# Natural head order, loads on two queues by time of use, unchained list scatters, a GpSimd mask and ranks by matmul in a DeltaNet block with routed experts

## The chip, the core and the metric

The kernel runs on one core of one Trainium2 chip. The metric is the device time of one execution in microseconds (us), as the median of several runs. A core has five engines with an instruction queue each: TensorE (PE in the profile; its weight loads are PEld), VectorE (DVE), ScalarE (ACT), GpSimd (POOL) and SyncE (SP), which here only issues DMAs. Each queue runs in order: an instruction that waits holds up all behind it, DMA issues included. DMAs move data between HBM and the on-chip SBUF; matmul results land in PSUM, from which VectorE and ScalarE copy them.

## The reference, cut to what matters

```python
def _attn_ref(q, k, v, beta):                     # B, H, S, D = 4, 8, 768, 48
    k_n = k / (np.linalg.norm(k, axis=-1, keepdims=True) + 1e-06)
    state = np.zeros((B, H, D, D))
    for t in range(S):
        y[:, :, t] = einsum('bhd,bhde->bhe', q[:, :, t], state)
        v_old = einsum('bhde,bhd->bhe', state, kt)
        state = state + bt * einsum('bhd,bhe->bhde', kt, vt - v_old)

# x = y in the order (B*S, H*D): 3072 tokens of 384
def _moe_ref(x, expert_emb, tau, w1, w2):         # E = 8 experts, F = 1024
    logits = xn @ en.T / tau                      # xn, en: rows over their norms
    expert_idx = np.argmax(logits, axis=1)
    gate_w = softmax(logits)[np.arange(N), expert_idx]
    for e in range(E):
        mask = expert_idx == e
        h = np.maximum(x[mask] @ w1[e], 0.0)
        out[mask] = gate_w[mask, None] * (h @ w2[e])
```

A delta-rule recurrence over 768 time steps gives 3072 tokens; each goes to the one expert whose embedding it is nearest to in angle.

## The kernel before, in words

Time is cut into 12 chunks of C = 64 steps. The four sequences are two pairs (`p`); a tile holds the two sequences of a pair in the two halves of its 128 partitions (`g`), 64 steps each, and the eight heads side by side.

For each chunk: `load` and `load_q` fetch keys (twice: `K` for the norms and products, `Kl` for the state update), values and queries; `squares`, `root`, `inverse_norms` and `unit_keys` scale the keys (GpSimd and VectorE); `transposes` puts keys and queries head by head on the partitions (TensorE, ScalarE); `products` multiplies the keys with keys and queries of the chunk (TensorE), and VectorE masks both to earlier steps into the tile `AP` (L263). The key products' 32-step diagonal blocks go through HBM (`blocks_out` L271, `blocks_in` L276) into `Bk`, one matrix per partition, for two chunks at once; `weigh` scales them by beta on GpSimd (L282); `eliminate` inverts the triangular matrices in 31 pairs of VectorE instructions (L290, L292), handed out a few at a time by `steps(n)`; `inverses_back` brings the inverses `Tk` back through HBM, `turn` transposes them, and `lower1` and `lower2` finish the 64-step inverse `W`. Then the recurrence itself: `residual` (values less what the state gives for the keys, L337 and L348), `solve` (with `W`, L357), `update` and `keep` (the state), `outputs`, `store`, and the router's `logits`.

The main loop runs c from -6 to 11 and is a hand-made pipeline under a manual schedule: in one iteration it works on norms of chunk c+6, products of chunk c+5, `lower1` and `lower2` of chunk c+1 and the recurrence of chunk c. Every two chunks share one reload and one elimination: the reload stands at the end of an even iteration, the elimination starts in the odd iteration behind it. What the source says first, each engine runs first. All loads and stores of this stage are issued by SP, in source order; ScalarE issues 16 small loads of beta at the start (L152).

After every fourth chunk `route` picks the experts of 1024 tokens in eight columns (`J`), as a generator of small steps that `fill(n)` advances: softmax, first maximum, then the place of each token in its expert's list: two matmuls give the ranks within a column (`mask_su`) and the counts of a column (`ones`), and eight pairs of VectorE additions carry the running count from column to column (L470, L471). Eight indirect DMAs from GpSimd (L482) scatter the token numbers into the list `idmap`; each is taken as depending on the one before it, since all write the same tensor.

Then the expert stage: 19 tiles of 256 list places. `fetch` reads a piece of `idmap` (L638), the expert's weights, and gathers the tokens (L646); `experts` multiplies (L657 to L670) and scatters the rows of the result. The first list read waits for all scatters.

Of the kernel before, what the change touches and what calls it, by code (L numbers as in the profile page):

```python
# [21 lines left out]
def kernel(  # L22
# [75 lines left out]
    run = cpool.tile([128, E], F32, name="run")  # L98
# [12 lines left out]
    for i in range(P2):  # L111
        Qs.append(ac.tile([128, NP, 2, 64], F32, name=f"Qp{i}"))
        nc.gpsimd.memset(Qs[i], 0.0)
        KNs.append(ac.tile([128, NP, 2, 64], F32, name=f"KN{i}"))
        nc.gpsimd.memset(KNs[i], 0.0)

    def heads(t):

        return t.rearrange("p (a b) d -> p b a d", a=2)

    def load(src, c, name, bufs):
        ts = []
        for p in range(P2):
            t = wk.tile([128, H, D], F32, name=name, tag=name, bufs=bufs)
            for g in range(2):
                nc.sync.dma_start(out=t[64 * g:64 * g + 64],
                                  in_=src[2 * p + g, :, c * C:(c + 1) * C, :].rearrange("h t d -> t h d"))
            ts.append(t)
        return ts

    def load_q(c):
        for p in range(P2):
            for g in range(2):
                for hh in range(2):
                    nc.sync.dma_start(out=Qs[p][64 * g:64 * g + 64, :, hh, 0:D],
                                      in_=q[2 * p + g, hh * NP:(hh + 1) * NP, c * C:(c + 1) * C, :]
                                      .rearrange("h t d -> t h d"))
# [5 lines left out]
    Kf[1] = load(k, 1, "K", 4)  # L143
# [83 lines left out]
    def unit_keys(c):  # L227
        for p in range(P2):
            nc.gpsimd.tensor_tensor(KNs[p][:, :, :, 0:D], heads(Kf[c][p]),
                                    rns[c][:, p].rearrange("p (a b) -> p b a", a=2).unsqueeze(3)  # L230
                                    .broadcast_to([128, NP, 2, D]), op=ALU.mult)
        del Kf[c]
# [7 lines left out]
    def transposes(c, p, i):  # L240
        if i == 0:
            KQs[c, p] = wk.tile([128, NP, 2, 2, C], F32, name="KQ", tag="KQ", bufs=12)
        src = (KNs, Qs)[i][p]
        psT = bank("f", 3).rearrange("p (a n) -> p a n", a=NP)
        for hp in range(NP):
            nc.tensor.transpose(psT[:, hp], src[:, hp].rearrange("p a d -> p (a d)"), ident)  # L246
        nc.scalar.activation(KQs[c, p][:, :, :, i, :], psT.rearrange("p a (g t) -> p a g t", g=2), ACT.Copy)  # L247

    def products(c, p):

        if p == 0:
            APs[c] = wk.tile([128, P2, 2, NP, 2, C], F32, name="AP", tag="AP", bufs=6)
# [9 lines left out]
        for hh in range(2):  # L262
            nc.vector.tensor_tensor(APs[c][:, p, hh].rearrange("p a i t -> p (a i) t"),  # L263
                                    psG[hh].rearrange("p (a t) -> p a t", t=C),
                                    later.broadcast_to([128, 2 * NP, C]), op=ALU.mult)

    def blocks_out(c):
        s, i = c // 2, c % 2
        A = APs[c].rearrange("p a b c i t -> p (a b c) i t")
# [8 lines left out]
    def weigh(s):  # L278
        Tks[s] = wk.tile([128, Q, Q], F32, name="Tk", tag="Tk")
        nc.gpsimd.memset(Tks[s], 0.0)  # L280
        nc.gpsimd.tensor_copy(Tks[s].rearrange("p a b -> p (a b)")[:, 0:Q * Q:Q + 1], bb[:, s])
        nc.gpsimd.tensor_tensor(Bks[s], Bks[s], bb[:, s].unsqueeze(1).broadcast_to([128, Q, Q]), op=ALU.mult)  # L282
# [23 lines left out]
    def lower1(c):  # L306
# [4 lines left out]
        A = APs[c].rearrange("p a b c i t -> p (a b c) i t")  # L311
# [29 lines left out]
    def residual(c, p):  # L341
        V = Vl[c][p]
        if c == 0:
# [4 lines left out]
        nc.vector.tensor_tensor(heads(R), heads(V),  # L348
                                psK[:, 0:Dm].rearrange("p (b a d) -> p b a d", a=2, d=D), op=ALU.subtract)
# [12 lines left out]
    def update(c, p):  # L362
        for hp in range(NP):
            for g in range(2):
                for hh in range(2):
                    h = hh * NP + hp
# [9 lines left out]
    def outputs(c, p):  # L376
# [4 lines left out]
        for hp in range(NP):  # L381
            for hh in range(2):
                for g in range(2):
                    r = slice(64 * g, 64 * g + 64)
                    o = 2 * D * hp + D * hh
                    nc.tensor.matmul(psY[r, o:o + D], lhsT=A[r, p, hh, hp, 1, :], rhs=Zs[p][r, hh * NP + hp, :],
                                     start=(c == 0 and hp == 0 and hh == 0), stop=True, skip_group_check=True)
        if p == 0:
            xcs[c] = wk.tile([128, P2, Dm], F32, name="xc", tag="xc", bufs=3)
        nc.scalar.activation(xcs[c][:, p].rearrange("p (a b d) -> p b a d", a=2, d=D),  # L390
                             psY[:, 0:Dm].rearrange("p (b a d) -> p b a d", a=2, d=D), ACT.Copy)
# [30 lines left out]
    def route(b):  # L422
# [29 lines left out]
        psR = bank("f", 3)[:, 0:2 * J * E].rearrange("p (i a e) -> p i a e", i=2, e=E)  # L452
# [13 lines left out]
        rk = t("rk", [128, 2, J, E])  # L466
        nc.vector.tensor_copy(rk, psR)
# [5 lines left out]
        nc.vector.tensor_tensor(rk[:, 0], rk[:, 0], base_e.broadcast_to(be), op=ALU.add)  # L473
        nc.vector.tensor_tensor(rk[:, 0], rk[:, 0], oh, op=ALU.mult)
        yield
        slot = t("slot", [128, J])
        nc.vector.tensor_reduce(slot, rk[:, 0], axis=AX.X, op=ALU.add)
# [3 lines left out]
        for j in range(J):  # L481
            nc.gpsimd.indirect_dma_start(  # L482
                out=idmap[:, :], out_offset=bass.IndirectOffsetOnAxis(ap=slot_i[:, j:j + 1], axis=0),
                in_=tokid[:, b * RC + j // P2, j % P2:j % P2 + 1], in_offset=None)


    behind = []
# [20 lines left out]
    for c in range(-6, NC):  # L508
        cf, cn, cl = c + 5, c + 6, c + 1
        odd = c % 2 == 1  # L510
        if odd and 0 <= (c + 1) // 2 < NS:
            inverses_back((c + 1) // 2)
        if odd:
            elim = eliminate((c + 3) // 2) if 0 <= (c + 3) // 2 < NS else None
        if has(cn):
            squares(cn)
        if has(cl):
            if c < 0:
                Kl[cl], Vl[cl] = load(k, cl, "Kl", 2), load(v, cl, "V", 4)
# [5 lines left out]
        if has(c):  # L525
            Rs = [residual(c, p) for p in both]
# [9 lines left out]
        if has(c):  # L536
            solve(c, 1, Rs[1])
        if has(cf):
            products(cf, 0)
        steps(3)  # L540
        if has(cn):
            inverse_norms(cn)
            unit_keys(cn)
            load_q(cn) if cn > 0 else None
        if has(cn + 2):
            Kf[cn + 2] = load(k, cn + 2, "K", 4)
        if has(c + 2) and c + 1 >= 0:
            Kl[c + 2], Vl[c + 2] = load(k, c + 2, "Kl", 2), load(v, c + 2, "V", 4)
# [3 lines left out]
        if has(cf):  # L552
            products(cf, 1)
            blocks_out(cf)
            if cf % 2 == 1:
                blocks_in(cf // 2)
                weigh(cf // 2)
# [4 lines left out]
        if odd and 0 <= (c + 1) // 2 < NS:  # L562
            turn((c + 1) // 2)
        fill(6)
        if has(c):
            outputs(c, 0)
            steps(3)
            fill(6)
# [41 lines left out]
    nc.vector.tensor_tensor(thr, run[0:1].unsqueeze(2).broadcast_to([1, E, N // T]), thr, op=ALU.is_gt)  # L610
# [23 lines left out]
    def fetch(i):  # L634
# [3 lines left out]
        nc.sync.dma_start(ids, idmap[bass.ds(s, T), :].rearrange("(p t) o -> p (t o)", t=2))  # L638
# [75 lines left out]
```

## Time and profile before

| | |
|---|---|
| median of 3 runs | 983.29 us (980.25 to 984.8) |
| the profiled execution | 983.6 us, its span 980.7 us |
| TensorE, weight loads | busy 718.4 and 577.7 us (73% and 59%) |
| VectorE, ScalarE, GpSimd | busy 277.0, 167.0 and 226.7 us (28%, 17%, 23%) |
| DMA | 109.57 MB in 197903 packets, mean 112 GB/s |
| mean granted TensorE clock | 0.824 |

The span runs from the first to the last instruction. Busy times are sums over stages with different limits, so a share of the whole span says little. In a timeline row stand the start, the duration, engine, line, operation, tile written and tiles read, and how many instructions were merged; in brackets how long the engine stood idle before it, and what ended that.

### The profile page before, as it was taken

What the parts mean: (1) busy time and instruction counts of PE and PEld (TensorE: products, weight loads), DVE (VectorE), ACT (ScalarE), POOL (GpSimd) and SP (SyncE); (2) the same over time, 40 slices, a digit from 0 to 9 for tenths busy, and PEclk for the clock granted to TensorE, in tenths of its full rate; (3) what the DMA queues carried; (4) which work ended last, traced back from release to release, by engine and by line L of the source; (5) the groups of instructions that cost most, each with busy time, mean ns of one, the idle gap of its engine ahead of it and who ended that gap; (6) DMA issues with size and microseconds to landing.
All of it is one profiled execution on the core that took longest, in us unless ns stands there. A gap on an engine that the chain in (4) does not pass through costs nothing. (4 is left out here: it accounts for less than half of the span.)

```text
span 980.7 us, 17338 instructions
## 1 busy us (share of the span) xinstructions
PE 718.4 (73%) x7305; PEld 577.7 (59%) x7305; DVE 277.0 (28%) x727; ACT 167.0 (17%) x330; POOL 226.7 (23%) x228
## 2 busy tenths in 40 slices
PE   0534476958280699896602999999999999999995
PEld 0423475848270599785501777776666666677773
DVE  2338754738430567520310000000001001100000
ACT  0211041423120243332200101101000000001110
POOL 3742524233202403022022111111111111211100
PEclk9956596777755787676755999999999999999998
DMA  3434745474330326303006654454555444555400
GB/s 58 74 78 103 124 84 115 81 145 86 81 63 6 63 58 146 73 2 67 17 0 233 201 170 161 155 172 155 178 181 178 158 159 155 171 182 185 153 0 0
DMA packets 197903, 109.57 MB, mean 112 GB/s; under 512 B 163329, under 2 KB 186041, under 8 KB 197826
## 3 DMA queue, kind: packets, MB, share of 16 engines
q1 hardware_dynamic: 190992, 96.00, 37.1%
q0 software_dynamic: 5632, 12.24, 4.4%
q8 instruction: 57, 0.93, 0.4%
q10 hardware_dynamic: 1202, 0.23, 0.1%
q14 instruction: 20, 0.16, 0.1%
HBM read 92.56 MB, written 18.63 MB: 113 GB/s over the span
## 5 line engine op out<-in xcount | busy, mean ns | idle before, releaser
L664 PE MATMUL two<-xTm,w 128*128 128x256 f32 x912 | 204.1, 384 | 12.4 <-DVE xTm L658 12.4
L670 PE MATMUL one<-w,hT 128*128 128x384 f32 x608 | 199.2, 486 | 0.0
L664 PEld LDWEIGHTS two<-xTm,w 128*128 128x128 f32 x912 | 173.2, 192 | 40.2 <-DVE xTm L658 17.0
L670 PEld LDWEIGHTS one<-w,hT 128*128 128x128 f32 x608 | 115.5, 190 | 76.5
L673 DVE TENSOR_SCALAR y<-one,xg 128x384 f32<-128x384 f32 x38 | 23.5, 618 | 390.2 <-PE one L670 390.2
L666 ACT ACTIVATE hT<-two 128x512 f32<-128x512 f32 x76 | 45.4, 598 | 431.1 <-PE two L664 431.1
L674 POOL DMA_INDIRECT out_dram<-y,ids x38 | 38.1, 1004 | 242.1 <-DVE y L673 242.1
L290 DVE TENSOR_TENSOR tmp<-Bk,Tk 128x31 f32<-128x31 f32 (+15 forms) x186 | 74.7, 401 | 5.0
L357 PE MATMUL r<-R,W 64*64 64x48 f32 x704 | 30.5, 251 | 59.8 <-DVE R L348 59.8
L292 DVE TENSOR_TENSOR Tk<-Tk,tmp 128x31 f32<-128x31 f32 (+15 forms) x186 | 68.2, 367 | 6.4
L646 POOL DMA_INDIRECT xg<-x_dram,ids x38 | 37.3, 982 | 134.6 <-DMA ids<-idmap 103.7
L357 PEld LDWEIGHTS r<-R,W 64*64 64x64 f32 x704 | 28.2, 167 | 63.7 <-DVE R L348 59.9
L259 PE MATMUL f<-KQ 48*64 48x128 f32 x768 | 39.0, 336 | 31.2 <-DVE AP L263 31.2
L657 PE MATMUL one<-ident,xg 128*128 128x128 f32 x114 | 20.4, 290 | 54.6 <-DMA xg<-x_dram,ids 47.7
L482 POOL DMA_INDIRECT idmap<-tokid,slot_i x24 | 23.5, 981 | 129.9 <-DMA idmap<-tokid,slot_i 69.6
L259 PEld LDWEIGHTS f<-KQ 48*64 48x64 f32 x768 | 31.5, 170 | 35.0 <-DVE AP L263 32.8
L657 PEld LDWEIGHTS one<-ident,xg 128*128 128x128 f32 x114 | 13.6, 145 | 65.1 <-issue 50.7
L337 PE MATMUL r<-S,KQ 128*64 128x96 f32 x704 | 50.6, 312 | 0.0
L326 PE MATMUL f<-Wd,PI 64*64 64x32 f32 x768 | 38.4, 272 | 16.2 <-ACT PI L318 16.1
L326 PEld LDWEIGHTS f<-Wd,PI 64*64 64x64 f32 x768 | 36.9, 198 | 19.3 <-ACT PI L318 18.3
L337 PEld LDWEIGHTS r<-S,KQ 128*64 128x64 f32 x704 | 43.0, 181 | 2.4 <-issue 1.0
L247 ACT ACTIVATE KQ<-f 128x512 f32<-128x512 f32 x48 | 27.8, 597 | 88.9 <-PE f L246 88.5
(123 smaller groups left out, 653.8 us busy)
## 6 DMA issues: line engine op xcount, KB each, us to landing
w<-in_moe_w_dram SPq DMA_DIRECT2D x38, 1536.0 KB
K<-in_k_dram SPq DMA_DIRECT2D x48, 96.0 KB
Qp<-in_q_dram SPq DMA_DIRECT2D x96, 48.0 KB
Kl<-in_k_dram SPq DMA_DIRECT2D x48, 96.0 KB
V<-in_v_dram SPq DMA_DIRECT2D x48, 96.0 KB
x_dram<-xc SPq DMA_DIRECT2D x24, 192.0 KB
a_dram<-AP SPq DMA_DIRECT2D x48, 64.0 KB
Bk<-a_dram SPq DMA_DIRECT2D x6, 512.0 KB
```

The source lines that it names most:

```text
L259: nc.tensor.matmul(psG[hh][64 * g:64 * g + 64, 128 * hp:128 * hp + 128], lhsT=KQ[r, hp, g, 0, :], rhs=KQ[r, hp, g, :, :], start=True, stop ...
L290: nc.vector.tensor_tensor(tv, Bk[:, i, i + 1:Q].unsqueeze(2).broadcast_to(sh), Tk[:, i:i + 1, 0:i + 1].broadcast_to(sh), op=ALU.mult)
L292: nc.vector.tensor_tensor(Tk[:, i + 1:Q, 0:i + 1], Tk[:, i + 1:Q, 0:i + 1], tv, op=ALU.subtract)
L326: nc.tensor.matmul(psW[r, m, :], lhsT=PI[r, m, :], rhs=Wds[s][r, n + m, :], start=True, stop=True, skip_group_check=True)
L337: nc.tensor.matmul(ps1[64 * g:64 * g + 64, 2 * D * hp:2 * D * (hp + 1)], lhsT=KQs[c, p][:, hp, g, i, :], rhs=state(c, p)[:, g, hp].rearran ...
L357: nc.tensor.matmul(psZ[r, h, :], lhsT=Ws[c][r, p * H + h, :], rhs=R[r, h, :], start=True, stop=True, skip_group_check=True)
L646: nc.gpsimd.indirect_dma_start(out=x, out_offset=None, in_=x_dram[:, :], in_offset=bass.IndirectOffsetOnAxis(ap=ids[:, t:t + 1], axis=0))
L657: nc.tensor.transpose(psX[:, j, :], xg[t][:, j * 128:(j + 1) * 128], ident)
L664: nc.tensor.matmul(psH[:, 0, i * T:(i + 1) * T], lhsT=w1[:, j, (f + i) * 128:(f + i + 1) * 128], rhs=xT[:, j, :], start=(j == 0), stop=(j ...
L666: nc.scalar.activation(hT[:, f:f + 2, :], psH[:, 0].rearrange("p (i t) -> p i t", i=2), ACT.Relu)
L670: nc.tensor.matmul(psO, lhsT=hT[:, f, t * 128:(t + 1) * 128], rhs=w2[:, f, :], start=(f == 0), stop=(f == NF - 1))
L674: nc.gpsimd.indirect_dma_start(out=out[:, :], out_offset=bass.IndirectOffsetOnAxis(ap=ids[:, t:t + 1], axis=0), in_=y, in_offset=None, bou ...
```

## The change

In words:

- Heads are kept in their natural order: a pair of heads on the partitions of a transposed tile is (2h, 2h+1), not (h, h+4). Queries of a half tile are loaded by one DMA instead of two; the rearranging views at residual and output go.
- Loads move in the source: keys for the norms one iteration ahead at the top of the iteration, values right behind them, queries behind the solve. The second key load `Kl` is issued by ScalarE, one iteration ahead, behind the solve. `blocks_out` now stands with no load between it and the products in SP's queue.
- `weigh` moves from the end of the even iteration to the top of the odd one, its part that needs no reload becomes `diagonal`. `residual` comes ahead of `squares`. `inverse_norms` and `unit_keys` come behind the second products.
- VectorE masks only the key products; ScalarE copies the query products unmasked into `AP`, and a new GpSimd step `causal` masks them there.
- The column counts are summed by matmul: eight matmuls with `ones` over shrinking widths and one with `mask_su` add up in one PSUM tile, so two VectorE additions replace the sixteen.
- The scatters of a list are declared independent of one another, with a one-element memset between them; every list read is made to wait for all of them.
- `fill` advances the router by 4 small steps at two places where it took 6.

The diff, cut to its core:

```diff
+    def by_token(src, c, b):
+        return src[b, :, c * C:(c + 1) * C, :].rearrange("h t d -> t h d")
+    def load(src, c, name, bufs, queue=nc.sync):
...
+                queue.dma_start(out=t[64 * g:64 * g + 64], in_=by_token(src, c, 2 * p + g))
     def load_q(c):
...
-                for hh in range(2):
-                    nc.sync.dma_start(out=Qs[p][64 * g:64 * g + 64, :, hh, 0:D],
+                nc.sync.dma_start(out=Qs[p][64 * g:64 * g + 64, :, 0:D], in_=by_token(q, c, 2 * p + g))
...
         for hh in range(2):
-            nc.vector.tensor_tensor(APs[c][:, p, hh].rearrange("p a i t -> p (a i) t"),
-                                    psG[hh].rearrange("p (a t) -> p a t", t=C),
-                                    later.broadcast_to([128, 2 * NP, C]), op=ALU.mult)
+            A = APs[c][:, p, hh:H:2]
+            G = psG[hh].rearrange("p (a i t) -> p a i t", i=2, t=C)
+            nc.vector.tensor_tensor(A[:, :, 0], G[:, :, 0], later.broadcast_to([128, NP, C]), op=ALU.mult)
+            nc.scalar.activation(A[:, :, 1], G[:, :, 1], ACT.Copy)
+    def causal(c, p):
+        nc.gpsimd.tensor_tensor(APs[c][:, p, :, 1], APs[c][:, p, :, 1], later.broadcast_to([128, H, C]), op=ALU.mult)
...
-        for i, w in enumerate((mask_su, ones)):
-            nc.tensor.matmul(psR[:, i], lhsT=w, rhs=ohf, start=True, stop=True, skip_group_check=True)
+        for j in range(J):
+            nc.tensor.matmul(psR[:, (j + 1) * E:], lhsT=ones, rhs=ohf[:, 0:(J - j) * E],
+                             start=(j == 0), stop=False, skip_group_check=True)
+        nc.tensor.matmul(psR[:, 0:J * E], lhsT=mask_su, rhs=ohf, start=False, stop=True, skip_group_check=True)
...
-        for j in range(J):
-            nc.vector.tensor_tensor(rk[:, 0, j], rk[:, 0, j], run, op=ALU.add)
-            nc.vector.tensor_tensor(run, run, rk[:, 1, j], op=ALU.add)
-            yield
+        nc.vector.tensor_tensor(rk, rv[:, 0:J], run.broadcast_to(be), op=ALU.add)
+        nc.vector.tensor_tensor(run, run, rv[:, J:J + 1], op=ALU.add)
...
+            tc.declare_no_dep(put, group="places", reason="each token has a place of its own")
+            tc.add_to_no_dep_group("places", put)
+            puts.append(put)
+            nc.gpsimd.memset(between, 0.0)
```

The main loop after the change, from its top to the second products and on:

```python
    if back is not None: inverses_back(back)
    if has(cn + 1): Kf[cn + 1] = load(k, cn + 1, "K", 4)
    if c == -1:
        Vl[0] = load(v, 0, "V", 4)
        Kl[0] = load(k, 0, "Kl", 2, nc.scalar)
    if has(c + 2) and c >= -1: Vl[c + 2] = load(v, c + 2, "V", 4)
    if odd and 0 <= (c + 3) // 2 < NS:
        weigh((c + 3) // 2)
        elim = eliminate((c + 3) // 2)
    if has(c): Rs = [residual(c, p) for p in both]
    if has(cn): squares(cn)
    ...                                   # kl, root, kl, transposes, steps(3), solve as before
    if has(cl + 1) and cl >= 0: Kl[cl + 1] = load(k, cl + 1, "Kl", 2, nc.scalar)
    if has(cn) and cn > 0: load_q(cn)
    if has(cf): products(cf, 0)
    steps(3)
    ...                                   # update
    if has(cf):
        products(cf, 1); blocks_out(cf); causal(cf, 0)
        if cf % 2 == 1: blocks_in(cf // 2)
    if has(cn): inverse_norms(cn); unit_keys(cn)
    if has(cf):
        causal(cf, 1)
        if cf % 2 == 1: diagonal(cf // 2)
    ...                                   # keep, steps(3), turn, fill(4), outputs, steps(3), fill(4), ...
```

## Rows read from the trace of the kernel before

**Rows 1.** Windows, expert stage: busy time and count per engine, granted clock, DMA share, GB/s

```profile
600.00:700.00 100.00, 94.83 (x375) 68.39 (x374) 10.67 (x19) 9.56 (x16) 17.79 (x18) 1.00 0.50 165
```

**Rows 2.** Waits of TensorE, 30 to 470 us: total us, times, longest us

```profile
PE r L357 <- DVE R L348: 59.8, 4, 33.7
PE f L259 <- DVE AP L263: 31.2, 5, 13.0
PE f L455 <- DVE oh L450: 22.9, 2, 18.6
PE S L368 <- POOL kl L237: 9.3, 1, 9.3
```

**Rows 3.** Timeline, end of iteration c=0 and start of c=1

```profile
133.05 1.22 DVE L263 TENSOR_TENSOR AP<-f,later 128x512 f32<-128x512 f32 x2
...
143.38 2.20 SPq L271 DMA_DIRECT2D a_dram<-AP  x4
147.19 0.34 SPq L276 DMA_DIRECT2D Bk<-a_dram  x1
...
151.07 2.34 POOL L282 TENSOR_TENSOR Bk<-Bk,bb 128x1024 f32<-128x1024 f32 x1 [14.87 <-DMA Bk<-a_dram]
...
156.08 1.95 PE L357 MATMUL r<-R,W 64*64 64x48 f32 x32 [13.73 <-DVE R L348]
```

**Rows 4.** Timeline, scatters in c=5 and at the end, first list reads and gathers

```profile
289.05 1.22 POOL L482 DMA_INDIRECT idmap<-tokid,slot_i  x1 [20.97 <-DVE slot_i L479]
...
322.16 1.61 POOL L214 TENSOR_TENSOR Ksq<-K 128x384 f32<-128x384 f32 x2
...
490.13 1.06 POOL L482 DMA_INDIRECT idmap<-tokid,slot_i  x1 [8.54 <-DVE ends L616]
...
518.57 0.96 POOL L482 DMA_INDIRECT idmap<-tokid,slot_i  x1 [2.12 <-DMA idmap<-tokid,slot_i]
522.43 0.38 SPq L638 DMA_DIRECT2D ids<-idmap  x1
...
527.30 0.96 POOL L646 DMA_INDIRECT xg<-x_dram,ids  x1 [0.30 <-issue]
```

**Rows 5.** Timeline, starts of the residuals of c=1 to c=6

```profile
138.82 1.54 PE L337 MATMUL r<-S,KQ 128*64 128x96 f32 x32
...
180.04 2.83 PE L337 MATMUL r<-S,KQ 128*64 128x96 f32 x32
...
200.78 1.54 PE L337 MATMUL r<-S,KQ 128*64 128x96 f32 x32
...
239.52 2.83 PE L337 MATMUL r<-S,KQ 128*64 128x96 f32 x32
...
286.13 2.83 PE L337 MATMUL r<-S,KQ 128*64 128x96 f32 x32
...
348.84 2.83 PE L337 MATMUL r<-S,KQ 128*64 128x96 f32 x32
```

**Rows 6.** Timeline, the first blocks that are written out

```profile
43.47 1.22 DVE L263 TENSOR_TENSOR AP<-f,later 128x512 f32<-128x512 f32 x2
...
51.28 2.87 SPq L271 DMA_DIRECT2D a_dram<-AP  x4
```

**Rows 7.** Timeline: ScalarE's loads at the start; one VectorE step alone and beside GpSimd

```profile
0.81 12.30 ACTq L152 DMA_DIRECT2D bb<-in_beta_dram  x16
...
139.01 0.34 DVE L290 TENSOR_TENSOR tmp<-Bk,Tk 128x175 f32<-128x175 f32 x1
...
167.34 0.96 DVE L290 TENSOR_TENSOR tmp<-Bk,Tk 128x175 f32<-128x175 f32 x1
```

**Rows 8.** Groups by line: operation, shapes, count, busy us, mean ns, idle before

```profile
L263 DVE TENSOR_TENSOR AP<-f,later 128x512 f32<-128x512 f32 x48 | 30.2, 672 | 30.5 <-PE f L259 30.5
...
L237 POOL TENSOR_TENSOR kl<-Kl,rn 128x384 f32<-128x384 f32 x24 | 20.2, 846 | 29.1 <-DMA Kl<-in_k_dram 28.7 <-PE f L316 0.4
...
L360 ACT ACTIVATE Z<-r 128x384 f32<-128x384 f32 x24 | 11.8, 491 | 99.1 <-PE r L357 99.1
```

More of the change, by code (lines that the diff above doesn't have):

```diff
@@ L97 @@
         nc.gpsimd.iota(tokid[64 * g:64 * g + 64], pattern=[[C, NC], [2 * S, P2]], base=g * S, channel_multiplier=1)
-    run = cpool.tile([128, E], F32, name="run")
+    run = cpool.tile([128, 1, E], F32, name="run")
     nc.vector.memset(run, 0.0)
@@ L142 @@
     load_q(0)
-    Kf[1] = load(k, 1, "K", 4)
     Kl, Vl = {}, {}
@@ L251, in products @@
         if p == 0:
-            APs[c] = wk.tile([128, P2, 2, NP, 2, C], F32, name="AP", tag="AP", bufs=6)
+            APs[c] = wk.tile([128, P2, H, 2, C], F32, name="AP", tag="AP", bufs=6)
         KQ = KQs[c, p]
@@ L276, in blocks_in, with diagonal @@
         nc.sync.dma_start(out=Bks[s], in_=a_dram[s % 2].rearrange("b i n s t -> (b i n) s t"))
-    def weigh(s):
+    def diagonal(s):
         Tks[s] = wk.tile([128, Q, Q], F32, name="Tk", tag="Tk")
@@ L281, in weigh @@
         nc.gpsimd.tensor_copy(Tks[s].rearrange("p a b -> p (a b)")[:, 0:Q * Q:Q + 1], bb[:, s])
+    def weigh(s):
         nc.gpsimd.tensor_tensor(Bks[s], Bks[s], bb[:, s].unsqueeze(1).broadcast_to([128, Q, Q]), op=ALU.mult)
@@ L510 @@
         odd = c % 2 == 1
[L511 to L514, printed above, removed]
+        back = (c + 1) // 2 if odd and 0 <= (c + 1) // 2 < NS else None
+        if back is not None:
+            inverses_back(back)
+        if has(cn + 1):
+            Kf[cn + 1] = load(k, cn + 1, "K", 4)
+        if c == -1:
+            Vl[0] = load(v, 0, "V", 4)
+            Kl[0] = load(k, 0, "Kl", 2, nc.scalar)
+        if has(c + 2) and c >= -1:
+            Vl[c + 2] = load(v, c + 2, "V", 4)
+        if odd and 0 <= (c + 3) // 2 < NS:
+            weigh((c + 3) // 2)
+            elim = eliminate((c + 3) // 2)
+        if has(c):
+            Rs = [residual(c, p) for p in both]
         if has(cn):
@@ L524 @@
             unit_keys_again(cl, 1)
-        if has(c):
-            Rs = [residual(c, p) for p in both]
         if has(cf):
@@ L537 @@
             solve(c, 1, Rs[1])
+        if has(cl + 1) and cl >= 0:
+            Kl[cl + 1] = load(k, cl + 1, "Kl", 2, nc.scalar)
+        if has(cn) and cn > 0:
+            load_q(cn)
         if has(cf):
@@ L540 @@
         steps(3)
[L541 to L548, printed above, removed]
         if has(c) and c < NC - 1:
@@ L554 @@
             blocks_out(cf)
+            causal(cf, 0)
             if cf % 2 == 1:
                 blocks_in(cf // 2)
-                weigh(cf // 2)
+        if has(cn):
+            inverse_norms(cn)
+            unit_keys(cn)
+        if has(cf):
+            causal(cf, 1)
+            if cf % 2 == 1:
+                diagonal(cf // 2)
         if has(c) and c < NC - 1:
@@ L561 @@
         steps(3)
-        if odd and 0 <= (c + 1) // 2 < NS:
-            turn((c + 1) // 2)
-        fill(6)
+        if back is not None:
+            turn(back)
+        fill(4)
         if has(c):
@@ L567 @@
             steps(3)
-            fill(6)
+            fill(4)
             outputs(c, 1)
@@ L637, in fetch @@
         ids = mk.tile([128, 2], I32, name="ids", tag="ids", bufs=4)
-        nc.sync.dma_start(ids, idmap[bass.ds(s, T), :].rearrange("(p t) o -> p (t o)", t=2))
+        got = nc.sync.dma_start(ids, idmap[bass.ds(s, T), :].rearrange("(p t) o -> p (t o)", t=2)).ins
+        for put in puts:
+            tc.add_manual_dep(got, put.name, mybir.DependencyInfo(mybir.DependencyClass.Sync, mybir.DependencyReason.DATA),
+                              reason="all tokens are in their places")
         w1 = wt.tile([128, KC, F], F32, name="w1", tag="w1")
```

55 lines of the change are left out of this document (22 added, 33 removed).

## The prediction

> **What bounds the kernel now.** I read the windows first. [...]
>
> (a) The reload. In every second iteration `weigh` on GpSimd waits for the reload of `Bk`, and behind it on the same queue stand the squares of the keys, then on VectorE their sums, and behind those the residual that TensorE's solve needs. In c=1 GpSimd waited 14.87 us and TensorE 13.73 [rows 3]. The reload is late because its writes are: the product tile was masked by 134.27 (133.05 + 1.22), but the writes were issued at 143.38, behind twelve loads in SP's queue [rows 3].
>
> (b) The scatters. Each list scatter waits for the landing of the one before: eight take from 490.13 to 518.57, 4.06 apart, and the first list read goes out only at 522.43 [rows 4]. In c=5 the same eight hold GpSimd from 289.05 to 322.16 [rows 4], and TensorE waits 33.7 us for the residual [rows 2]. The second batch shows, in c=10, as the 9.3 us wait for `kl`.
>
> (c) The router of the first batch sits in c=4 with its square root behind `weigh`: 18.6 of the 22.9 us on `oh` [rows 2].
>
> So iterations differ: by the starts of the residuals, c=1 took 41.2 us, c=2 20.7, c=3 38.7, c=4 46.6 and c=5 62.7 [rows 5]. An undisturbed one is near 21.
>
> **The change part by part.** *The tail.* Eight scatters without the chain: two gathers in a row are issued 0.30 + 0.95 = 1.25 us apart [rows 4], and a one-element memset adds some 0.1, so I take 1.4. Bounds: 1.25, and 4.06 if something else paces them. The last scatter starts 7 x (4.06 - 1.4) = 18.6 us earlier, and its landing and the first list read with it. The ranks lose a copy and 14 of 16 small VectorE additions in a row and gain seven matmuls in a row; I take these as equal, and 1.5 us either way as the bound. **-18.6.**
>
> *Start (c=-6 to -1).* Key norms and products are ordered as before. The first reload's writes went out at 51.28, though the tile was masked at 44.69 [rows 6]; they now follow the mask, which itself comes about a microsecond earlier, ahead of the inverse norms and on half the columns. The elimination follows them by some 8 us; for the second reload I take 4 more, since its queue was shorter; from nothing to 6.6 is possible. At c=-1 ScalarE's new loads cost 1 (below). **-11**, with bounds -6 and -15.
>
> *Even iterations.* SP loses four query loads and the four key reloads, but these are issued by ScalarE, at 12.30 / 16 = 0.77 us each [rows 7]: 3.1 us in front of its two new copies. A ScalarE copy of 384 columns takes 0.49 [rows 8], so 256 columns about 0.4. TensorE's second products need the banks that those copies release: 3.1 + 0.8 = 3.9 later at most, zero if ScalarE's idle time takes it. Part of it TensorE spent on its own matmuls and the first mask anyway; I take **+2.3 each**. VectorE's half mask goes from 0.67 to about 0.4, 48 times, 13 us in all; it counts for little, as the TensorE chain sets these iterations.
>
> *The GpSimd mask.* 384 columns take 0.85 there [rows 8], so 512 take 1.13, 24 times. A VectorE step of 175 columns takes 0.34 alone and 0.96 while GpSimd multiplies [rows 7]: about 0.6 per GpSimd operation, 24 x 0.6 = 14 us, what the half masks gave back. Net nothing by that row; the bounds are nothing lost to the masks (-13) and the whole of 24 x 1.13 = 27 lost (+13). [...]
>
> *Odd iterations.* After the change the residual no longer waits for GpSimd; the reload gates only the elimination. From the end of the mask: writes landed 143.38 to 147.19, 3.8; reload 147.19 to 151.07, 3.9; `weigh`, squares and sums 4.5 (the restart of TensorE at 156.08 is 5.0 behind, with the residual in it) [rows 3]: 12.2. Of this 4.55 (134.27 to 138.82 [rows 3, 5]) plus the 2.3 above lie in the even iteration, so the steps start 5.35 behind the residual. The rest of the iteration took 24.0 (156.08 to 180.04). About 5 of it, the solve and the first products, now run under the reload. About 3 come back on ScalarE: its key loads need the buffers that `kl` frees, and `kl` stands on GpSimd behind `weigh`, squares and root; ScalarE's copies, the state copies and the second products queue behind that wait. So 5.35 + 22 = 27.3: c=1 -13.9, c=3 -11.4, with +2.3 for c=0 and c=2: **-20.7**. The bounds are the full price of ScalarE's wait (8 us: nearly nothing won in c=3) and none of it.
>
> *c=4.* The router's root no longer stands behind `weigh`, but behind two masks, the unit keys and a memset, near 5 us of GpSimd work; with nothing ahead the same matmuls waited 4.3 in c=8 (22.9 - 18.6 [rows 2]). So 18.6 becomes 9.3 to 10; less the 2.3 and about 1 for the matmuls: **-6**.
>
> *c=5.* Eight scatters now take 11.2 in place of 33.1 [rows 4]. They start 2.9 behind the residual or a little earlier, `weigh` follows at some 13.5, the steps at 18, the end 22 later: 40 in place of 62.7. **-22.7**.
>
> *c=6 to c=10.* ScalarE's loads: +2.3 and +1 in c=6 and c=7. In c=9 ScalarE waits behind the eight scatters for its buffers: +7. In c=10 the 9.3 goes, with about 2 of matmuls at the low clock behind it. **-1**.
>
> Sum: 18.6 + 11 + 20.7 + 6 + 22.7 + 1 = 80. The profiled execution took 983.6 with a span of 980.7, so the sum gives 900.7 + 2.9 = 903.6; the median of the runs is 0.3 lower. I predict 903.
>
> **The rivals.** *ScalarE's waits cost nothing, and TensorE keeps the high clock.* It idles enough: 99 us of waiting ahead of its `Z` copies alone [rows 8]. Against it: its queue is in order. Then the evens lose their 2.3 (9), the odd ones 3 each (9), c=9 its 7, c=4 and the start some 8: 903 - 33 = 870. Chance 0.24.
>
> *The scatters keep their pace*, because landings or a ring and not the semaphore set it. Nothing in the rows shows scatters in flight together. Then 18.6 is lost at the end, 21 in c=5 and some 3 in c=9: 946. Chance 0.1.
>
> *The stall only changes place*: the steps, and with them the products, wait in the odd iterations as long as the residual did, because GpSimd and ScalarE now wait for each other. The 20.7 go, and a few of the start: 928. Chance 0.14.
>
> *The masks hold VectorE for their whole length*: the +13 above, if its steps always meet them; against it, half of each iteration VectorE has other work or none. 903 + 13 = 916. [...] Chance 0.06.
>
> *Slower than before*: ScalarE, with its key loads in the middle of its stream, becomes the serial resource of each iteration. It is slower when that wait holds TensorE 80 / 12 = 6.7 us longer than I count in every iteration from c=-1 to c=10. In the odd ones this can be (8 us of GpSimd work stand ahead of the buffers); in the even ones the waiting work is done before `Z`. At 8 us each: 903 + 96 = 999. Chance 0.03.
>
> **How the numbers follow.** The forecast holds 0.41, with a range of its own from 885 to 920; 0.02 is left for other causes. From 866 to 938 lie the forecast, most of the first rival, the third and the masks: 0.41 + 0.17 + 0.14 + 0.06, near 8 in 10. A measurement of this kernel tells 0.5% (5 us) from no change. Faster by more has 0.41 + 0.24 + 0.1 + 0.14 + 0.06 and half of the rest, 0.96; same 0.01; slower 0.03.
>
> **What would show it.** Scatters 1.3 to 1.5 apart and the first list read near 11 us behind the first of them (tail); TensorE's waits for the residual and on `oh` gone or halved, and in their place waits for ScalarE's copies in odd iterations (forecast) or none (first rival); writes of blocks right behind the mask; VectorE's steps longer beside GpSimd's mask; residual starts near 23 and 27 us apart by turns. The prediction is wrong if scatters still come 4 us apart, if TensorE waits as long for the products as it did for the residual, or if the expert stage itself, about 458 us, changes.

## The result, and the profile after

The changed kernel takes 949.33 us (median of 4 runs, 940.29 to 951.07) against 982.79 for the kernel before on the same chip: a ratio of 0.964, 95% interval 0.958 to 0.971. It is faster by some 33 us. I had said 903, with 866 to 938 as the range. The profiled execution took 949.2 us, its span 947.5; before it was 980.7, so 33.2 us of span have to be found. In the ratios of this document a run that is over 1.5% above the fastest of its kernel is left out (one run of number 1, one of number 5 and two of the four of number 11), while the medians hold all runs.

First TensorE's waits, from 30 to 470 us, in the same columns as [rows 2]:

```profile
PE f L252 <- ACT AP L259: 39.7, 11, 13.4
PE S L366 <- issue: 18.8, 12, 8.8
PE f L454 <- DVE den L458: 14.6, 2, 10.2
PE f L325 <- ACT PI L317: 10.9, 4, 5.4
...
PE r L355 <- issue: 7.4, 8, 1.1
PE f L454 <- DVE oh L447: 5.8, 1, 5.8
PE r L336 <- issue: 4.7, 1, 4.7
```

The 59.8 us on the residual and the 9.3 on `kl` of [rows 2] are gone. The wait for the products' banks has moved from VectorE to ScalarE and grown from 31.2 to 39.7. New is "issue", 31 us on three lines: TensorE stood still and the profile shows nothing that it waited for. The waits on `den` and `oh` are the router's: 10.2 us in c=4, where it was 18.6, and 5.8 in c=8, where it was 4.3; the other 4.4 belong to the third batch, which in the kernel before lies behind 470 us.

Then the timeline, the starts of the residuals of c=1 to c=6, c=9 and c=10, to be read against [rows 5]:

```profile
137.63 2.83 PE L336 MATMUL r<-S,KQ 128*64 128x96 f32 x32
...
166.62 2.80 PE L336 MATMUL r<-S,KQ 128*64 128x96 f32 x32
...
193.60 2.83 PE L336 MATMUL r<-S,KQ 128*64 128x96 f32 x32
...
220.54 2.83 PE L336 MATMUL r<-S,KQ 128*64 128x96 f32 x32
...
262.94 2.83 PE L336 MATMUL r<-S,KQ 128*64 128x96 f32 x32
...
309.15 2.82 PE L336 MATMUL r<-S,KQ 128*64 128x96 f32 x32
...
380.17 2.21 PE L336 MATMUL r<-S,KQ 128*64 128x96 f32 x32
...
425.28 2.83 PE L336 MATMUL r<-S,KQ 128*64 128x96 f32 x32
```

For c=9 and c=10 the kernel before has these starts:

```profile
416.80 2.83 PE L337 MATMUL r<-S,KQ 128*64 128x96 f32 x32
...
436.73 2.83 PE L337 MATMUL r<-S,KQ 128*64 128x96 f32 x32
```

Subtract neighbours and the span is accounted for:

| stretch | before | after | measured | forecast |
|---|---|---|---|---|
| start to c=1 | 138.8 | 137.6 | -1.2 | -8.7 (-11 and +2.3) |
| c=1 | 41.2 | 29.0 | -12.2 | -13.9 |
| c=2 and c=3 | 59.5 | 53.9 | -5.6 | -9.1 |
| c=4 | 46.6 | 42.4 | -4.2 | -6 |
| c=5 | 62.7 | 46.2 | -16.5 | -22.7 |
| c=6 to c=8 | 68.0 | 71.0 | +3.1 | +3.3 |
| c=9 | 19.9 | 45.1 | +25.2 | +7 |
| c=10 to the first scatter of the tail | 53.4 | 38.2 | -15.2 | -11.3 |
| first scatter to first list read | 32.3 | 25.4 | -6.9 | -18.6 |
| the rest (expert stage) | 458.3 | 458.7 | +0.4 | 0 |

Of the 46.8 us that are missing from my 80, 36 lie in three rows, c=5, c=9 and the tail: those in which scatters are in flight.

The tail after, to be read against [rows 4]:

```profile
463.43 1.06 POOL L481 DMA_INDIRECT idmap<-tokid,slot_i  x1 [8.45 <-DVE ends L631]
...
472.38 0.95 POOL L481 DMA_INDIRECT idmap<-tokid,slot_i  x1 [0.21 <-issue]
...
488.85 0.38 SPq L653 DMA_DIRECT2D ids<-idmap  x1
```

The eight are issued (472.38 - 463.43) / 7 = 1.28 apart, as forecast. But the first list read goes out 16.5 us behind the last of them, where it took 3.9 in [rows 4] (518.57 to 522.43). The issue got faster and the landing did not follow. The scatters' packets are not what takes so long: from 474.2 to 488.5 the profile has no DMA packet at all on any queue, and the list read still waits for the scatters to land.

And c=9, where eight scatters are issued from 381.74 to 391.67 while TensorE solves and updates:

```profile
390.45 0.33 PE L366 MATMUL S<-Z,kl 64*48 64x48 f32 x2 [0.48 <-issue]
390.72 0.95 POOL L481 DMA_INDIRECT idmap<-tokid,slot_i  x1 [0.22 <-issue]
...
397.19 0.31 PE L366 MATMUL S<-Z,kl 64*48 64x48 f32 x1 [1.50 <-issue]
...
401.72 0.59 PE L366 MATMUL S<-Z,kl 64*48 64x48 f32 x14 [4.22 <-issue]
...
410.85 1.39 PE L336 MATMUL r<-S,KQ 128*64 128x96 f32 x13 [4.68 <-issue]
```

While the scatters are issued TensorE advances by one to five matmuls at a time, and later it stands still for 4 us twice; the last stop ends 19 us after the last scatter was issued. In c=5 one such stop lasts 8.8 us (the longest in the waits above).

### The profile page after: what moved, and what is told of

It is laid out like the page before. It is cut to its first block, busy times and chain, and to the rows that moved or that the text cites. A ratio compares the mean times of both kernels' runs of the same rounds, so it can differ in the third digit from the quotient of the medians.

```text
span 947.5 us, 17416 instructions
## 1 busy us (share of the span) xinstructions
PE 734.4 (78%) x7347; PEld 590.8 (62%) x7347; DVE 276.9 (29%) x682; ACT 182.2 (19%) x378; POOL 260.9 (28%) x276
## 5 line engine op out<-in xcount | busy, mean ns | idle before, releaser
L682 PE MATMUL two<-xTm,w 128*128 128x256 f32 x912 | 204.8, 385 | 12.4 <-DVE xTm L676 11.7
L291 DVE TENSOR_TENSOR Tk<-Tk,tmp 128x31 f32<-128x31 f32 (+15 forms) x186 | 87.4, 470 | 6.4
L252 PE MATMUL f<-KQ 48*64 48x128 f32 x768 | 39.5, 328 | 41.4 <-ACT AP L259 39.7
L252 PEld LDWEIGHTS f<-KQ 48*64 48x64 f32 x768 | 30.8, 166 | 47.2 <-ACT AP L259 42.5
L336 PE MATMUL r<-S,KQ 128*64 128x96 f32 x704 | 53.2, 320 | 4.8 <-issue 4.7
L336 PEld LDWEIGHTS r<-S,KQ 128*64 128x64 f32 x704 | 44.6, 187 | 8.0 <-issue 6.6
L214 POOL TENSOR_TENSOR rn<-rn,half 128x16 f32<-128x16 f32 x12 | 35.3, 2941 | 39.7 <-DVE rn L211 39.7
L325 PE MATMUL f<-Wd,PI 64*64 64x32 f32 x768 | 37.1, 267 | 10.9 <-ACT PI L317 10.9
L262 POOL TENSOR_TENSOR AP<-AP,later 128x512 f32<-128x512 f32 x24 | 31.8, 1327 | 48.9 <-ACT AP L259 48.9
L325 PEld LDWEIGHTS f<-Wd,PI 64*64 64x64 f32 x768 | 35.6, 192 | 14.0 <-ACT PI L317 12.7
```

The lines of the kernel that those rows point to most:

```text
L214: nc.gpsimd.tensor_tensor(out=rns[c].rearrange("p a h -> p (a h)"), in0=rns[c].rearrange("p a h -> p (a h)"), in1=half, op=ALU.pow)
L252: nc.tensor.matmul(psG[hh][64 * g:64 * g + 64, 128 * hp:128 * hp + 128], lhsT=KQ[r, hp, g, 0, :], rhs=KQ[r, hp, g, :, :], start=True, stop ...
L291: nc.vector.tensor_tensor(Tk[:, i + 1:Q, 0:i + 1], Tk[:, i + 1:Q, 0:i + 1], tv, op=ALU.subtract)
L325: nc.tensor.matmul(psW[r, m, :], lhsT=PI[r, m, :], rhs=Wds[s][r, n + m, :], start=True, stop=True, skip_group_check=True)
L336: nc.tensor.matmul(ps1[64 * g:64 * g + 64, 2 * D * hp:2 * D * (hp + 1)], lhsT=KQs[c, p][:, hp, g, i, :], rhs=state(c, p)[:, g, hp].rearran ...
L682: nc.tensor.matmul(psH[:, 0, i * T:(i + 1) * T], lhsT=w1[:, j, (f + i) * 128:(f + i + 1) * 128], rhs=xT[:, j, :], start=(j == 0), stop=(j ...
```

## The experiments

All times are medians beside runs of the kernel before on the same chip. The median of before lay between 974.6 and 982.8 from chip to chip, so kernels of different groups are compared by their ratios to it; 0.01 is some 9.8 us. The changed kernel itself was run in the first group only.

| kernel | median us | ratio to before | 95% interval |
|---|---|---|---|
| the change | 949.33 | 0.964 | 0.958 to 0.971 |
| 1: without early scatters | 902.33 | 0.921 | 0.912 to 0.930 |
| 2: second batch chained | 946.83 | 0.968 | 0.964 to 0.973 |
| 3: places spread | 917.03 | 0.938 | 0.933 to 0.943 |
| 4: `Kl` on SP | 939.08 | 0.962 | 0.957 to 0.967 |
| 5: mask on VectorE | 933.47 | 0.952 | 0.944 to 0.959 |
| 6: early scatters one by one | 921.94 | 0.941 | 0.934 to 0.947 |
| 7: 3 and 6 together | 894.18 | 0.915 | 0.912 to 0.919 |
| 8: 3, 5 and 6 together | 881.19 | 0.903 | 0.899 to 0.907 |
| 9: 8 with `Kl` on SP | 888.39 | 0.909 | 0.904 to 0.913 |
| 10: before, places spread | 944.62 | 0.964 | 0.962 to 0.967 |
| 11: the change, all chained | 973.77 | 0.984 | 0.978 to 0.991 |

The theory with which I began: scatters in flight together pile up, their landings come late, and while they do everything else that must land waits too. The rival: the two load queues hold one another up. In c=5 SP's reload of the inverses stood 36 us behind a key load that ScalarE issues.

**1. Without early scatters.**

```diff
-        for j in range(J):
+        for j in range(J) if b == 2 else []:
             put = nc.gpsimd.indirect_dma_start(
```

> Left out: the sixteen list scatters of the first two batches (so two thirds of the tokens reach no expert; the number of tiles stays). Theory pile-up (eight scatters in flight at once hold up everything else that has to land, TensorE's instructions too): TensorE's waits on issue in c=5 and c=9 (18.8 us for L366, 7.4 for L355, 4.7 for L336) go; c=5 falls from 46 us to about 27, like c=3, c=9 from 45 to about 20, c=10 stays near 16: 949 - 44 = 905, between 895 and 915. Rival, the two load queues (SP and ScalarE wait for each other's loads: SP's reload of the inverses waited 36 us on a key load in c=5, its value load 28 us in c=9): only the 11 us that GpSimd spends issuing in c=5 go, c=9 stays near 45: 930 to 940. Both: tail unchanged, 25 us from the first scatter to the first list read.

It came to 0.921, 0.043 below the change: 42 us. The residual starts of c=4, c=5, c=6, c=9 and c=10 of this kernel, from its timeline:

```profile
220.51 2.83 PE L336 MATMUL r<-S,KQ 128*64 128x96 f32 x32
...
258.27 2.43 PE L336 MATMUL r<-S,KQ 128*64 128x96 f32 x32
...
285.61 2.83 PE L336 MATMUL r<-S,KQ 128*64 128x96 f32 x32
...
362.80 2.83 PE L336 MATMUL r<-S,KQ 128*64 128x96 f32 x32
...
379.90 1.54 PE L336 MATMUL r<-S,KQ 128*64 128x96 f32 x32
```

c=5 takes 27.3 instead of 46.2 and c=9 17.1 instead of 45.1. TensorE's waits on issue at L366, L355 and L336 are gone, while SP's loads still wait for ScalarE's key loads (60.9 us in 17 waits, against 55.2 in 12). Of the 28.0 us in c=9, 15.9 are time in which TensorE stood idle and 12.1 are the same 403 matmuls taking longer: the change's mean granted clock is 0.55 there, and the 64 matmuls of L325 take 3.63 us, against 2.06 in number 1. So the scatters are the cause of these stalls, and the two queues by themselves are not. The eight scatters that are left, unchained and neighbouring, land this long after their issue:

```profile
DMA to landing us min/median/max: 4.0/11.6/13.7
```

Sixteen early scatters cost the changed kernel 40 us and more, of which I had charged 11.2 us of GpSimd's time in c=5 and 7 us in c=9.

**2. The second batch chained again.**

```diff
+            if b != 1:
-            tc.declare_no_dep(put, group="places", ...)
+                tc.declare_no_dep(put, group="places", ...)
```

> Only the second batch's scatters (c=9) wait for each other's landing again. Pile-up: c=9 falls from 45 to about 20 us without waits of TensorE on issue, and c=10 grows from 16 to some 30, since its keys wait behind the chain on GpSimd as in the kernel before: about -10, 939. Rival, the two load queues: c=9 stays near 45 and c=10 grows all the same: 950 to 963.

Neither: 0.968 is level with the change within the intervals, where the theory had 10 us less; c=9 stays long, as the rival has it, but c=10 does not grow (37.9 us from 429.71 to the tail's first scatter at 467.61, after 38.2). c=9's solve and update now run without stops (only 1.8 us on issue are left from 383 to 437 us), as the theory has it, but c=9 is as long as ever, 47.9 us (381.81 to 429.71). The timeline shows where the time went:

```profile
414.76 0.96 POOL L481 DMA_INDIRECT idmap<-tokid,slot_i  x1 [3.21 <-DMA idmap<-tokid,slot_i]
415.78 1.62 POOL L230 TENSOR_TENSOR kl<-Kl,rn 128x384 f32<-128x384 f32 x2
416.64 2.70 ACTq L125 DMA_DIRECT2D Kl<-in_k_dram  x4
...
421.93 1.54 PE L406 MATMUL f<-ident,xc 128*128 128x128 f32 x6 [25.35 <-ACT xc L388]
```

The chain holds GpSimd until 415.78. Only then does `kl` free the buffers for ScalarE's key loads. ScalarE stands in front of those loads all the while with its copies behind it (the next one waits 32.2 us), and TensorE waits 25.35 us for one of them. In the kernel before, the chain cost TensorE nothing in c=9 (19.9 us); with loads on ScalarE that wait for GpSimd it does.

**3. The list's places spread.** The changed kernel with place s at 230 (s mod 128) + s div 128; the list read takes as many descriptors as before.

```diff
+        nc.vector.tensor_single_scalar(hi, slot_i, 7, op=ALU.arith_shift_right)
+        nc.vector.tensor_copy(hi_f, hi)
+        nc.vector.tensor_scalar_mul(slot, slot, float(NMAP // 128))
+        nc.vector.scalar_tensor_tensor(out=slot, in0=hi_f, scalar=float(1 - NMAP), in1=slot, ...)
+        nc.vector.tensor_copy(slot_i, slot)
...
-        dma_start(ids, idmap[bass.ds(s, T), :].rearrange("(p t) o -> p (t o)", t=2))
+        dma_start(ids, idmap.rearrange("(p n) o -> p (n o)", p=128)[:, bass.ds(s, 2)])
```

> The list's places are laid out so that neighbouring places lie 920 bytes apart instead of 4 (place s at 230 (s mod 128) + s div 128), with as many descriptors as before; five small VectorE instructions more per batch, about 1 us each time. Theory: the landings come 3 us apart because the scatters in flight write into the same few lines of memory. Then the landings follow the issues at 1.3 us, the first list read comes 12 to 14 us behind the first scatter instead of 25, and c=5 and c=9 lose most of their stall: 949 - 12 - 30 = 907, between 895 and 925. Rival: a scatter of 128 pieces takes 3 us to land wherever it writes: 25 us at the tail as before, 950.

It came to 0.938, 26 us below the change. Its tail:

```profile
445.57 1.06 POOL L488 DMA_INDIRECT idmap<-tokid,slot_i  x1 [9.33 <-DVE ends L638]
...
454.52 0.95 POOL L488 DMA_INDIRECT idmap<-tokid,slot_i  x1 [0.22 <-issue]
...
457.25 0.38 SPq L660 DMA_DIRECT2D ids<-idmap  x1
```

The first list read now follows the last scatter by 2.7 us and the first by 11.7: the number that I had forecast for the changed kernel ("near 11", or 32.3 - 18.6 = 13.7 by my sum), after an edit that only moves the addresses. So the late landing came with the neighbouring addresses: 16.5 us from the last issue to the list read there, 2.7 here. But c=5 takes 39.2 and c=9 28.0 us here (by the residual starts), so 23 of the 47 us that the first experiment removed from the two stay, and the timeline of c=9 shows TensorE advancing in small steps while GpSimd issues:

```profile
386.47 0.96 POOL L488 DMA_INDIRECT idmap<-tokid,slot_i  x1 [0.21 <-issue]
386.97 0.40 PE L366 MATMUL S<-Z,kl 64*48 64x48 f32 x3 [0.50 <-issue]
387.69 0.23 PE L366 MATMUL S<-Z,kl 64*48 64x48 f32 x1 [0.32 <-issue]
387.73 0.96 POOL L488 DMA_INDIRECT idmap<-tokid,slot_i  x1 [0.22 <-issue]
388.38 0.41 PE L366 MATMUL S<-Z,kl 64*48 64x48 f32 x3 [0.46 <-issue]
```

From 384.04 to 392.66 it does 27 matmuls, some four in the 1.27 us from one scatter to the next. The steps are 0.7 us apart, so they are not the scatters' own rhythm, and they end 1.4 us after the last scatter is issued (391.21). So a second thing is at work while scatters are issued in a row, apart from late landings.

**4. `Kl` on SP.**

```diff
-            Kl[cl + 1] = load(k, cl + 1, "Kl", 2, nc.scalar)
+            Kl[cl + 1] = load(k, cl + 1, "Kl", 2)
```

> The second key load is issued by SP again, at the same place in the source. Theory: ScalarE's four issues per iteration (2.7 to 5.4 us) stand in front of its copies of the products, TensorE waits for the banks (39.7 us on AP in all) and falls to the low clock behind it, and SP's other loads wait for ScalarE's (55 us in twelve iterations): c=0, c=2 and c=4 lose 4 to 6 us each, the odd ones 2 to 3: 949 - 22 = 927, between 918 and 936. Rival: SP then waits itself for the buffers that GpSimd frees, with the queries and the blocks behind it in its queue: within 5 us of 949, or up to 10 more.

Level (0.962): the rival. TensorE's wait on the AP copies falls as expected, from 39.7 to 24.7, and the wait on `PI` rises from 10.9 to 25.2 in its place; the start loses too, with the residual of c=1 at 146.70 instead of 137.63. From this kernel's waits of TensorE:

```profile
PE f L325 <- ACT PI L317: 25.2, 6, 16.1
PE f L252 <- ACT AP L259: 24.7, 5, 10.2
```

In this run and in number 9 nothing measurable in the whole time hangs on which of the two engines issues these loads: 0.962 against 0.964, and 0.909 against 0.903, with overlapping intervals both times.

**5. Mask on VectorE.**

```diff
-            nc.vector.tensor_tensor(A[:, :, 0], G[:, :, 0], later.broadcast_to([128, NP, C]), op=ALU.mult)
-            nc.scalar.activation(A[:, :, 1], G[:, :, 1], ACT.Copy)
+            nc.vector.tensor_tensor(A, G, later.unsqueeze(1).broadcast_to([128, NP, 2, C]), op=ALU.mult)
...
-            causal(cf, 0)
```

> VectorE masks both products in one instruction again, as before; no copies by ScalarE, no GpSimd mask. My prediction's term (GpSimd's mask and ScalarE's copies cost what VectorE's halves give back): within 5 us of the changed kernel, 944 to 954 (ratio to before 0.957 to 0.970). Rival: the wait of TensorE for the banks, 39.7 us on ScalarE's AP copies against 31.2 on VectorE's mask before, and VectorE's elimination steps, 470 ns instead of 367, are this split's doing: TensorE's wait on AP falls under 30 us, and the time by 10 to 20 us, 930 to 940.

It came to 0.952, 12 us below the change: the rival. Number 8 gives the same difference to number 7 again, so the rows are shown there.

**6 and 7. Early scatters one by one**, in the changed layout (6) and in the spread one (7). Each is gated by a one-element GpSimd copy that reads a result of the running iteration.

```diff
+    def put_one(gate):
+        if single:
+            nc.gpsimd.tensor_copy(between, gate)
+            single.pop(0)()
...
             Rs = [residual(c, p) for p in both]
+            put_one(Rs[0][0:1, 0, 0:1])
...
+            put_one(Zs[0][0:1, 0, 0:1])     # behind the solve; also Zs[1], and xcs[c] behind each output
```

> The sixteen scatters of the first two batches go out one by one, each behind a result of the running iteration (residual, solve, outputs), five in one iteration; places as in the changed kernel. Pile-up of landings theory: with some 5 us between two, each lands (3 us) before the next: c=5 about 27 to 30, c=9 about 21: 949 - 38 = 911, between 903 and 920. Rival (it is the scatters' total work in memory, not their crowding, that delays the rest): within 10 us of 949.

> Places 920 bytes apart (as in the third experiment) and the early scatters one by one. In the third experiment TensorE still advanced only four or five matmuls per scatter while GpSimd issued eight in a row, although their landings came 1.3 us apart. Theory: it is the issuing in a row that does this; one by one it goes, and c=4 to c=5, c=5 and c=9 together lose the 23 us that they still had over the run without early scatters: 917 - 20 = 897. Rival: each scatter costs TensorE the same wherever it stands: 912 to 920. Against the paced one without spread places: 12 us less at the tail under both.

6 gained 23 us of the 38 that I expected (0.941); c=5 and c=9 fall to 29.2 and 22.3, but c=10 grows from 38.2 to 43.3, and the tail stays at 24.6 (441.54 to 466.18). 7 came to 0.915, 22 us below number 3, with 20 expected: once early scatters are neither neighbours nor issued in a row, the waits on issue leave TensorE's list, and c=5 and c=9 take 27.9 and 17.1, as without any scatter.

**8. And the mask on VectorE.** The edits of 3, 5 and 6 together.

> As the one above, with the mask on VectorE as in the kernel before. By my term for the mask: within 5 us of the one above. By its rival: 10 to 20 us less, near 882. The combination is the candidate to beat both kernels.

881.19 us, ratio 0.903: faster than both kernels, 12 us below number 7. TensorE's wait on the banks, from the waits of number 7:

```profile
PE f L252 <- ACT AP L259: 42.0, 12, 13.5
```

and from the waits of number 8:

```profile
PE f L252 <- DVE AP L258: 26.8, 7, 9.3
```

What VectorE got for its half masks is in the groups by line. The changed kernel's:

```profile
L291 DVE TENSOR_TENSOR Tk<-Tk,tmp 128x31 f32<-128x31 f32 (+15 forms) x186 | 87.4, 470 | 6.4
L289 DVE TENSOR_TENSOR tmp<-Bk,Tk 128x31 f32<-128x31 f32 (+15 forms) x186 | 74.9, 403 | 5.0
...
L258 DVE TENSOR_TENSOR AP<-f,later 128x256 f32<-128x256 f32 x48 | 18.1, 418 | 38.7 <-PE f L252 28.5 <-remote 10.2
```

Number 8's:

```profile
L290 DVE TENSOR_TENSOR Tk<-Tk,tmp 128x31 f32<-128x31 f32 (+15 forms) x186 | 75.7, 407 | 6.4
L288 DVE TENSOR_TENSOR tmp<-Bk,Tk 128x31 f32<-128x31 f32 (+15 forms) x186 | 75.3, 405 | 7.5 <-POOL Bk L280 2.5
...
L258 DVE TENSOR_TENSOR AP<-f,later 128x512 f32<-128x512 f32 x48 | 30.8, 683 | 18.6 <-PE f L252 18.6
```

The half masks save VectorE 12.7 us (30.8 to 18.1), and its elimination steps beside GpSimd's mask take 11.3 more (162.3 against 151.0; number 7, which differs from number 8 by the mask alone, has 162.1). That is the "net nothing" that I worked out. What I had priced too low is what the split does to TensorE: from number 8 to number 7 it waits 15.2 us longer for its banks, now on ScalarE's copies. The experiment takes those copies and GpSimd's mask out together, so it does not show which of the two delays them.

**9. Number 8 with `Kl` on SP.** The edit is that of number 4.

> The eighth experiment's kernel with the second key load issued by SP again. In the second experiment ScalarE stood 30 us behind its own key loads, whose buffers GpSimd had not freed. Theory: without a late GpSimd ScalarE's four issues (2.7 to 5 us an iteration) still stand in front of its copies; on SP they go, 10 to 15 us less: 868 (ratio 0.888 to 0.895). Rival, as the fourth experiment came out level: SP pays it back with queries and blocks that wait behind the key loads, above all at the start: within 5 us of 881, or up to 8 more.

0.909 and overlapping intervals: not faster, the rival again. Here too the wait moves to `PI` (25.8 us).

**10. The kernel before with nothing but the places spread.** The edit is that of number 3; the chain stays.

> The kernel before with nothing changed but the places, 920 bytes apart; the scatters still wait for each other. Theory (a scatter's 128 pieces hold one another up where they share lines of memory): each lands about 2.5 us behind its issue instead of 4, the eight come 2.6 apart instead of 4.06, the tail loses 10 to 11 us, c=5 about 10, c=10 some 6 to 9: ratio to before 0.968 to 0.975. Rival (only several scatters in flight collide, one alone lands in 4 us wherever it writes): 0.998 to 1.003.

0.964, a little more than the theory gave, and the ratio of the whole change. From issue to landing a scatter takes, in the kernel before:

```profile
DMA to landing us min/median/max: 2.8/3.9/5.5
```

and in number 10:

```profile
DMA to landing us min/median/max: 2.1/2.1/3.6
```

Its scatters in c=5, from the timeline:

```profile
288.76 1.21 POOL L489 DMA_INDIRECT idmap<-tokid,slot_i  x1 [21.86 <-DVE slot_i L486]
...
303.73 0.96 POOL L489 DMA_INDIRECT idmap<-tokid,slot_i  x1 [1.44 <-DMA idmap<-tokid,slot_i]
306.12 0.96 POOL L489 DMA_INDIRECT idmap<-tokid,slot_i  x1 [1.43 <-DMA idmap<-tokid,slot_i]
307.11 1.61 POOL L214 TENSOR_TENSOR Ksq<-K 128x384 f32<-128x384 f32 x2
```

Even one scatter alone lands sooner: the next is issued 2.4 us behind it and not 4 or more [rows 4], and GpSimd is free after 18.4 us in place of 33.1. So the addresses count within one scatter too, 3.9 against 2.1 us by the median; what makes neighbouring pieces slower no run shows.

**11. The change with all scatters chained.**

```diff
-            tc.declare_no_dep(put, group="places", reason="each token has a place of its own")
-            tc.add_to_no_dep_group("places", put)
```

> The changed kernel with all scatters waiting for each other again: what the unchaining alone was worth. From the second experiment: tail 7 us more, c=9 about 7 more (ScalarE behind its key loads, whose buffers GpSimd frees late), c=5 with GpSimd held for 33 us instead of 11 and ScalarE behind it, some 15 more: 949 + 29 = 978, ratio to before about 0.994. Rival, if the crowd of unchained scatters cost as much as the chain: within 5 us of 949, ratio 0.960 to 0.969.

0.984, between 0.978 and 0.991: the four runs lie far apart (959.57 to 979.26), and this is the least certain of the ratios. So unchaining by itself was worth some 0.020, 20 us, and by the two intervals between 11 and 29: the 29 that I expected here is not excluded, but it is well below the 52.6 that my terms for the tail, c=5 and c=10 had given it (18.6, 22.7 and 11.3). All the rest of the change together was worth some 0.016.

## Why the prediction was wrong, step by step

**The step that failed** stands in *The tail*: "The last scatter starts 18.6 us earlier, and its landing and the first list read with it." The scatters did come 1.3 apart; the landing did not come with them. It followed the last issue by 16.5 us in place of 3.9, and 11.7 of the 18.6 were lost. The same step is at work in *c=5*, where I charged eight scatters with the 11.2 us that GpSimd takes to issue them, and in *c=9*. Without them c=5 takes 27.3 and c=9 17.1 (number 1): they cost 18.9 and 28.0. I had the chain's 4.06 us per scatter in front of me and took all of it for the price of waiting. Number 10 shows that the addresses are part of it: with the places spread, the chained scatters follow each other at 2.4 us. With the places spread and the scatters unchained (number 3) the terms come out nearly as forecast: c=5 takes 39.2 where I had 40, c=9 28.0 where I had 26.9, the first list read comes 11.7 behind the first scatter where I had 13.7. In c=9 that is luck, since I had ScalarE wait there and it is TensorE that is slowed. What the prediction lacked is that eight neighbouring scatters in flight land late: 11.6 us behind their issue by the median in number 1, where a chained one takes 3.9 in the kernel before.

The rival that keeps the scatters' pace gave 946, 3 us from the result, and I gave it 0.1. Of the causes that it names, late landings are what the tail shows: 16.5 us from the last issue to the list read, with the issues 1.28 apart. Elsewhere it had the right sum by luck, for another reason: it charged 21 us in c=5 and 3 in c=9 to a GpSimd that is held up, where 6.2 and 18.2 were lost against my forecast, with GpSimd free after 10 us and TensorE standing still.

For the same bytes the list read goes out 16.5 us behind the last issue with neighbouring places, and 2.7 with spread ones in the same memory (number 3). A scatter lands 3.9 us behind its issue by the median with neighbouring places and the chain (the kernel before), 11.6 without the chain (number 1), and 2.1 with spread places and the chain (number 10).

**Right.** The two waits that I wanted gone are gone (residual, `kl`). c=1 gave 12.2 of 13.9. The router's wait in c=4 is 10.2 us, after a forecast of 9.3 to 10. The ranks are worth nothing: from the last step on `oh` to `slot_i` the tail takes 5.9 us (457.04 to 462.97) after 6.0 before (483.66 to 489.67). The expert stage is unchanged (458.7 us after 458.3). GpSimd's mask costs VectorE nearly what its half masks give back (11.3 us of 12.7).

**Right in kind, wrong in size.** The start: the writes that complete the first reload go out at 46.13 in place of 51.28, so 5.2 earlier (they are the second four, and not the first blocks as [rows 6] says, which went out at 39.88), and the first elimination starts 6.7 earlier (57.68 for 64.36); 5.3 is still there at c=0's first copy of keys (117.08 for 122.35), so the further 4 that I took for the second reload did not come; by c=1 1.2 is left, since c=0 gave back 4 and not 2.3. ScalarE's wait behind its loads was in the sum at 3 us for the odd iterations, and as a rival at 8. Chained scatters show what it can come to: 25.35 us on one copy (number 2).

**Mis-sized: the split of the mask.** I put 0.8 us for ScalarE's two new copies into each even iteration, and nothing into the others. TensorE's wait for the banks grew to 39.7, and putting the whole mask back on VectorE saves 12 us (numbers 5 and 8).

**Left open.** Why TensorE advances only some four matmuls per scatter while GpSimd issues eight in a row, with no wait that the profile shows. That it ends 1.4 us after the issuing is shown (number 3), and that it does not come when the scatters go one by one (number 7, 17.1 us in c=9); what gives way is not. Nor is it shown why TensorE stops for 4 to 8.8 us behind unchained neighbouring scatters. One candidate, untested: the packets of the two DMA queues that the profile marks as instruction (78 in all) may land late as well. The one that starts at 279.9, at the stop in c=5, took 2.9 us, where those of the kernel before from c=5 to c=9 take up to 1.8, but it ended 6 us before TensorE went on.

c=2 and c=3 together give 5.6 of 9.1; for one of them alone I would not read anything into its length, since the kernel of number 1, the same in that stretch, has 24.0 and 29.2 where the change has 27.0 and 26.9. The same holds for c=4: 42.4 us in the change at a granted clock of 0.66, 37.8 in number 1, where the 64 matmuls of L315 take 2.05 us and not 3.62.

## What to carry to other kernels

Taking the dependency out of a chain of DMAs brought the issues closer together here (4.06 to 1.28 us), and what it won beyond that hung on the landings (16.5 us from the last issue to the list read, 2.7 with the places spread): look at what the next one waited for before, and at the addresses that it writes. Small pieces that went to neighbouring addresses did better spread (0.938 against 0.964), and issued one at a time between other work (0.915 with both). And before loads are put on a computing engine's queue, find what frees their buffers: where that was late, so were the copies behind the loads, and TensorE waited 25.35 us for one (number 2).

## What the runs showed of the hardware that I had not expected

- A scatter of 128 pieces of 4 bytes lets the next go 4.06 us behind it when the places are neighbours [rows 4], and 2.39 when they lie 920 bytes apart (number 10; 303.73 to 306.12). With eight in flight the list read that waits for all of them goes out 25.4 us behind the first issue (the change) and 11.7 (number 3).
- While neighbouring scatters were outstanding, TensorE stopped for up to 8.8 us with nothing to wait for in the profile; in c=9 the last stop ended 19 us after the last issue.
- Eight scatters issued 1.27 us apart slowed TensorE to some four matmuls per scatter even with spread places (number 3); one or two at a time did not (number 7: c=9 in 17.1 us, no wait on issue at L336, L355 or L366).
